# Block-recurrent cross attention and a token-mixing MLP in one kernel: a new operation order, a block diagonal written by small DMAs, and fewer dummy matmuls

## The chip, the cores and the metric

The kernel runs on one core of a Trainium2 chip. The metric is the device time of one execution in microseconds (us); a profile's span is 1.7 to 2.2 us shorter than the time of the same execution (88.75 and 87.0 us in the profiled run before). The kernel before takes 88.36 us (median of 3 runs, 88.14 to 88.51). Runs of one kernel scatter: an execution is called slow when it lies over 1.5% above the fastest of its kernel, and ratios use the others, the fast ones.

## The reference, cut to what matters

```python
# x: (8 batches, 8 heads, 512 tokens, 64), state: (8, 8, 32, 64), all float32
scores  = scale * x @ state^T ; a  = softmax(scores)  ; xread = a  @ state   # tokens read the state
scores2 = scale * state @ x^T ; a2 = softmax(scores2) ; sread = a2 @ x       # the state reads the tokens
y = heads side by side of concat([xread, sread], tokens)    # (8, 544, 512)
wq = y @ w_q ; wk = y @ w_k                                 # (8, 544, 64)
out = relu(scale2 * (wq @ wk^T) @ y) @ w_out                # (8, 544, 512)
```

The kernel never forms `y`. It uses `wq (wk^T y)`: a 64 x 512 matrix `V` per batch, whose block-diagonal factors `stbd` (the state) and `sbd` (the state's read) appear below.

## The kernel before

One long list, `ORDER`, fixes the order in which the operations are issued; each token is operation, batch, and engine or tile mode (`v` VectorE, `a` ACT, which is ScalarE, `p` GpSimd; `t`, `c`, `r`: one 128-column matmul, two of 64 columns, four of 32). The parts that the change and the argument touch:

```python
def load(n, b, e):                     # "ix3": batch 3's x, 512 KB as bf16, asked for by GpSimd
    if n == "iwo":
        nc.gpsimd.dma_start(out=w_o, in_=moe_w_out.rearrange("(k p) e -> p k e", p=128))
    # ... "is": the state of batches 3 to 7
    else:
        b = int(n[2:])
        nc.gpsimd.dma_start(out=x_bf[b], in_=xsrc(b, 0, H))

def fill(n, b, e):                     # b dummy matmuls that cover waits
    ps = psA.tile([128, 512], FP, name="fill_ps", tag="psA")
    for w in range(b):
        nc.tensor.matmul(out=ps, lhsT=zero[:, 0:128], rhs=zero, start=True, stop=True)

def stbd_blk(n, b, e):                 # block diagonal of one batch's state, on GpSimd
    for r in range(2):
        nc.gpsimd.tensor_tensor(out=stbd[:, b, r],
            in0=st_bf[:, b, r : r + 1, :].to_broadcast((128, NP, D)),
            in1=mask[:, :, None].to_broadcast((128, NP, D)), op=ALU.mult)

def sw_mm(n, p, e):                    # state times w_q and w_k, 64 rows contracted
    # ... for bb, q, r:
        nc.tensor.matmul(out=ps[NS * q : NS * q + NS, r, 2 * DH * bb : 2 * DH * bb + 2 * DH],
            lhsT=stT[64 * r : 64 * r + 64, 2 * p + bb, r, NP * r + q, :],
            rhs=w_qk[64 * r : 64 * r + 64, q, 0:2, :], start=True, stop=True)

def srd(n, b, e):                      # the state's read: 32 matmuls of 32 columns each
    for r in range(2):
        for c in range(NC):
            for q in range(NP):
                nc.tensor.matmul(out=L[b]["srd"][NS * q : NS * q + NS, r, 0:D],
                    lhsT=L[b]["E"][:, r, c, q, :],
                    rhs=x_bf[b][:, NP * r + q, D * c : D * c + D],
                    start=False, stop=(r == 1 and c == NC - 1), skip_group_check=True)
```

Other names used below: `xT` transposes x, `pt` are the scores, `at` transposes the normalised scores `A`, `mix` and `mixs` are the mixed tokens and state rows, `fin` and `fix` the output matmuls of the tokens, `fs` those of the state rows of four batches.

The softmax here doesn't subtract the row's maximum and nothing guards it: scores larger than these inputs give would overflow.

Of the kernel before, what the change touches and what calls it, by code (L numbers as in the profile page):

```python
# [8 lines left out]
FP = mybir.dt.float32  # L9
# [31 lines left out]
wke.6.a wqe.6.v mix1.5.r ve.4.a mixs.5.r mix0.5.r mxe1.5.v sums.3.t mxe0.5.a g.6.t srd.3.r mixs.4.r
# [6 lines left out]
mse.0.a wke.7.v fin0.6.c wqe.7.a mxe0.3.a g.7.c fin1.6.c ge.7.a fin0.3.c oe0.6.v fin1.3.c os0.6.s  # L48
v.7.c oe0.3.a fin2.3.c ve.7.a fin3.3.c os0.3.s mix0.7.r oe1.3.a mixs.7.r fs.3.t mxe0.7.v mse.7.a
os1.3.s mix1.7.r fse.3.v fs.7.t mxe1.7.a fse.7.v fix1.7.t fix2.7.t oc1.7.a fix0.7.t oc2.7.a fix3.7.t  # L50
oc0.7.a oc3.7.b
"""


@with_exitstack
def kernel(
# [9 lines left out]
    nc = tc.nc  # L66
# [601 lines left out]
```

## Time and profile before

| | before |
|---|---|
| time, median of 3 | 88.36 us |
| span of the profiled run | 87.0 us |
| TensorE busy | 93% of the span |
| TensorE's share of the chain that ended last | 90% |
| matmuls plus weight loads in the profile | 3151 |
| dummy matmuls in `ORDER` | 23 |

The chain is the work followed back from the last instruction, at each step to what released it. The prediction below shows the lines that carry this and says how to read them. One row also belongs here. It stands in the page's table of DMA queues (queue, kind: packets, megabytes, share of 16 engines' span):

```profile
q8 instruction: 12, 0.20, 0.9%
```

Instructions come by DMA too: 12 packets of 16,384 B in the whole run. With a share of 0.9% they look like nothing.

### The profile page before, as it was taken

The numbers are of one execution on the slowest core, as the hardware profiler recorded it, in microseconds if no ns is written. First come the engines' busy times: TensorE is split into PE (matmuls) and PEld (weight loads), VectorE is DVE, ScalarE is ACT, GpSimd is POOL, SyncE is SP. The second block draws the span as 40 slices with busy tenths as digits, with TensorE's granted clock in tenths as the row PEclk, the third lists the DMA queues.
The fourth block names the chain that finished last, engine by engine and source line by source line (L and its number), as shares of the span: only waits on it lengthen the run. The fifth ranks groups of instructions, "written<-read, shape, count | busy, mean of one in ns | idle before, by whom it ended". The sixth has DMA issues, their size and how long they took to land.

```text
span 87.0 us, 3553 instructions
## 1 busy us (share of the span) xinstructions
PE 80.8 (93%) x1572; PEld 53.4 (61%) x1579; DVE 52.4 (60%) x111; ACT 55.9 (64%) x83; POOL 45.1 (52%) x58
## 2 busy tenths in 40 slices
PE   4999999999999999999999999999999999999910
PEld 1326666878777778777689747866755565544400
DVE  2125793997956875897856957891688264056010
ACT  1541637999898858778797838967930592665530
POOL 7999948999999969408507735327150000000000
PEclk9999999999999999999999999999999999999996
DMA  0899999999609999995600464201461663566782
GB/s 12 292 312 187 202 191 198 195 165 147 96 0 121 143 128 277 322 169 72 241 8 4 171 281 175 115 8 53 188 243 45 275 281 136 213 269 277 294 314 80
DMA packets 15119, 15.00 MB, mean 172 GB/s; under 512 B 3712, under 2 KB 12672, under 8 KB 15104
## 3 DMA queue, kind: packets, MB, share of 16 engines
q0 software_dynamic: 9104, 4.36, 39.7%
q1 hardware_dynamic: 4880, 8.98, 28.0%
q10 hardware_dynamic: 1120, 1.44, 4.6%
q8 instruction: 12, 0.20, 0.9%
q14 instruction: 3, 0.02, 0.1%
HBM read 10.22 MB, written 8.91 MB: 220 GB/s over the span
## 4 chain that ended last, share of the span: by engine, by line
PE 90%; ACT 4%; issue 1%; DVE 1%
PE fin_ps L161 20%; PE fin_ps L163 12%; PE fill_ps L155 6%; PE xT_ps L174 5%; PE mix_ps L541 5%; PE warm_ps L132 4%; PE srd_ps L369 3%; PE xT_ps L170 3%; PE at_ps L174 3%; PE v_ps L505 3%; PE pt_ps L163 2%; PE g_ps L163 2%; PE fins_ps L163 2%; PE wq_ps L433 2%; PE v_ps L514 2%; PE wk_ps L163 2%
## 5 line engine op out<-in xcount | busy, mean ns | idle before, releaser
L346 POOL TENSOR_TENSOR A<-E,rinv 128x1024 bf16<-128x1024 bf16 (+1 forms) x9 | 15.4, 1717 | 12.8 <-DVE rinv L340 12.5
L161 PE MATMUL fin_ps<-w_o,rmix 128*64 128x512 bf16 x160 | 19.4, 380 | 0.0
L142 ACT COPY ost<-fin_ps 128x1024 f32<-128x1024 f32 (+2 forms) x13 | 11.2, 864 | 11.6 <-PE fin_ps L161 5.9
L148 ACT ACTIVATE rmix<-mix_ps 128x1024 bf16<-128x1024 f32 x12 | 12.1, 1024 | 2.4 <-PE mix_ps L541 2.4
L407 POOL TENSOR_TENSOR sbd<-srn,mask 128x256 bf16<-128x256 bf16 x16 | 9.4, 614 | 6.0 <-DVE srn L397 5.9
L144 DVE COPY ost<-fin_ps 128x1024 f32<-128x1024 f32 (+1 forms) x6 | 6.5, 1091 | 9.9 <-PE fin_ps L163 5.4
L161 PEld LDWEIGHTS <-rmix 128*64 128x64 bf16 x160 | 8.4, 110 | 6.2 <-issue 0.6
L332 DVE TENSOR_REDUCE rsum<-E 128x16 f32<-128x512 bf16 x16 | 10.8, 676 | 0.9 <-ACT E L317 0.6
L163 PE MATMUL fin_ps<-w_o,rmix 128*128 128x512 bf16 x44 | 11.0, 379 | 0.2
L317 ACT ACTIVATE E<-pt_ps 128x512 bf16<-128x512 f32 x16 | 9.5, 601 | 2.5 <-PE pt_ps L161 1.3
L142 ACT COPY xT<-xT_ps 128x1024 bf16<-128x1024 bf16 x7 | 7.1, 1012 | 4.6 <-PE xT_ps L174 3.9
L234 POOL TENSOR_TENSOR stbd<-st_bf,mask 128x256 bf16<-128x256 bf16 x16 | 9.3, 610 | 0.4 <-DVE st_bf L144 0.2
L155 PE MATMUL fill_ps<-zero 128*128 128x512 bf16 x21 | 7.8, 432 | 0.1
L144 DVE COPY xT<-xT_ps 128x1024 bf16<-128x1024 bf16 x9 | 6.2, 690 | 2.7 <-PE xT_ps L174 2.5
L150 DVE TENSOR_SCALAR rmix<-mix_ps 128x1024 bf16<-128x1024 f32 x4 | 4.9, 1222 | 3.4 <-PE mix_ps L541 3.4
L163 PEld LDWEIGHTS <-rmix 128*128 128x128 bf16 x48 | 4.3, 98 | 4.0 <-ACT rmix L148 0.2
L183 POOL DMA_DIRECT2D x_bf<-in_x_dram x7 | 6.6, 949 | 0.0
L174 PE MATMUL xT_ps<-ident,x_bf 128*128 128x128 bf16 x80 | 6.0, 219 | 0.2 <-ACT E L317 0.2
L174 PEld LDWEIGHTS <-x_bf 128*128 128x128 bf16 x80 | 5.1, 98 | 1.3 <-issue 0.5
L541 PE MATMUL mix_ps<-wq,V 64*128 64x256 bf16 x64 | 5.8, 272 | 0.0
L132 PE MATMUL warm_ps<-zero 128*128 128x512 bf16 x8 | 3.6, 631 | 1.2 <-DVE mask L133 1.2
L163 PE MATMUL pt_ps<-stT,xT 128*128 128x64 bf16 x88 | 4.4, 193 | 0.0
(90 smaller groups left out, 139.7 us busy)
## 6 DMA issues: line engine op xcount, KB each, us to landing
out_dram<-ost SPq DMA_DIRECT2D x14, 512.0 KB, 2.8
x_bf<-in_x_dram POOLq DMA_DIRECT2D x7, 512.0 KB, 7.8
out_dram<-ost ACTq DMA_DIRECT2D x3, 256.0 KB, 2.1
x_f<-in_x_dram ACTq DMA_DIRECT2D x2, 256.0 KB, 4.0
x_f<-in_x_dram SPq DMA_DIRECT2D x2, 256.0 KB, 4.4
w_o<-in_moe_w_out_dram POOLq DMA_DIRECT2D x1, 512.0 KB, 8.4
out_dram<-ost SPq DMA_DIRECT2D x2, 256.0 KB, 2.4
st_bf<-in_state_dram POOLq DMA_DIRECT2D x1, 160.0 KB, 7.8
```

The source lines that it names most:

```text
L142: nc.scalar.copy(out=out, in_=in_)
L144: nc.vector.tensor_copy(out=out, in_=in_)
L148: nc.scalar.activation(out=out, in_=in_, func=AF.Relu)
L155: nc.tensor.matmul(out=ps, lhsT=zero[:, 0:128], rhs=zero, start=True, stop=True)
L161: nc.tensor.matmul(out=out[64 * h : 64 * h + 64], lhsT=lh, rhs=rhs, **kw)
L163: nc.tensor.matmul(out=out, lhsT=lhsT, rhs=rhs, **kw)
L174: nc.tensor.transpose(out=out, in_=in_, identity=ident)
L317: nc.scalar.activation(out=L[b]["E"][:, r].rearrange("p c q n -> p c (q n)"), in_=L[b][f"pt{r}"], func=AF.Exp, scale=float(scale),)
L332: nc.vector.reduce_sum(out=L[b]["rsum"][:, w], in_=L[b]["E"].rearrange("p r c q n -> p (r c q) n")[:, w], axis=AX.X,)
L346: eng.tensor_tensor(out=L[b]["A"].rearrange("p r c q n -> p (r c q) n")[:, w], in0=L[b]["E"].rearrange("p r c q n -> p (r c q) n")[:, w], ...
L407: nc.gpsimd.tensor_tensor(out=L[b]["sbd"][:, r], in0=L[b]["srn"][:, r : r + 1, :].to_broadcast((128, NP, D)), in1=mask[:, :, None].to_broa ...
L541: nc.tensor.matmul(out=ps[:, h, kk, :], lhsT=L[b]["V"][rows, 128 * k : 128 * k + 128], rhs=L[b]["wq"][rows, 0:SH], start=True, stop=True,)
```

## The change

The intent is to take work off TensorE (fewer dummy matmuls, fewer changes of tile shape) and off GpSimd (the block diagonal of batches 1 to 7), in an order searched anew. The diff, with the order cut to its first lines:

```diff
 ORDER = """
-fill.7.t xT0.0.t xc2.0.v xTe0.0.a fill.1.t xT1.0.t is.0.p stc.1.v fill.1.t stt.1.c xTe1.0.v stbd.2.p
-fill.1.t pt0.0.t stf.1.v fill.1.t pt1.0.t exp0.0.a ste.1.v iwo.0.p exp1.0.a rs0.0.v fill.4.t
-sums.0.t ix3.0.p rinv0.0.v wc.0.a ...            # ix4 stands after stbd.1 and stbd.6
+fill.5.t xT0.0.t xc2.0.v fill.1.t xT1.0.t xTe0.0.v is.0.p xTe1.0.v fill.1.t pt0.0.t iwo.0.p exp0.0.a
+stc.1.v fill.1.t pt1.0.t ix3.0.p sbs.0.s fill.1.t stt.1.c exp1.0.a rs0.0.v stf.1.a rinv0.0.v
+fill.2.t sums.0.t rs1.0.v A0.0.p ...             # ix4 stands right after sbd.0
 ... (all further lines of the order differ)
+    nc.vector.memset(stT.bitcast(FP), 0.0)
     def zeros(n, b, e):
-        nc.gpsimd.memset(stT.bitcast(FP), 0.0)
+        nc.gpsimd.memset(stbd[:, 1:B].bitcast(FP), 0.0)
+
+    def stbd_put(n, g, e):                        # "sbs": the block diagonal by DMA
+        b0, b1 = ((1, 3), (3, B))[g]
+        for q in range(NP):
+            rows = slice(NS * q, NS * q + NS)
+            nc.sync.dma_start(out=stbd[rows, b0:b1, :, q, :], in_=st_bf[rows, b0:b1])
 ...
-                        lhsT=stT[64 * r : 64 * r + 64, 2 * p + bb, r, NP * r + q, :],
-                        rhs=w_qk[64 * r : 64 * r + 64, q, 0:2, :],
+                        lhsT=stT[:, 2 * p + bb, r, NP * r + q, :],
+                        rhs=w_qk[:, q, 0:2, :],
```

More of the change, by code (lines that the diff above doesn't have):

```diff
@@ L16 @@
 ORDER = """
-zst.0.p ix1.0.p stc.0.v xc1.0.a fill.1.t stt.0.c ste.0.v stbd.0.p stf.0.a xc0.0.p xc3.0.v ix2.0.p
-fill.7.t xT0.0.t xc2.0.v xTe0.0.a fill.1.t xT1.0.t is.0.p stc.1.v fill.1.t stt.1.c xTe1.0.v stbd.2.p
-fill.1.t pt0.0.t stf.1.v fill.1.t pt1.0.t exp0.0.a ste.1.v iwo.0.p exp1.0.a rs0.0.v fill.4.t
-sums.0.t ix3.0.p rinv0.0.v wc.0.a fill.1.t xT0.1.t rs1.0.v fill.1.t srd.0.r xTe0.1.v A0.0.p fill.1.t
-xT1.1.t fill.1.t sw.0.r xTe1.1.a rinv1.0.v fill.1.t pt0.1.t srn.0.v A1.0.p at0.0.t srT.0.t exp0.1.a
@@ L22 @@
-pt1.1.t srTe.0.v sbd.0.p swe.0.a xT0.2.t rs0.1.v at1.0.t exp1.1.a xT1.2.t xTe0.2.v stbd.1.p ate.0.a
-xTe1.2.v fill.1.t stt.2.c stt.3.c rs1.1.v ste.2.a pt0.2.t stbd.6.p stf.3.v exp0.2.a fill.1.t wq.0.c
-ste.3.v wks.0.c ix4.0.p stf.2.a wk.0.t rs0.2.v sw.3.r pt1.2.t wke.0.v swe.3.a stbd.3.p sw.1.r
-rinv.1.v exp1.2.a g.0.t sw.2.r ge.0.v stbd.5.p swe.1.a rs1.2.v sums.2.t v.0.c wqe.0.a rinv.2.v
-xT1.3.c swe.2.a A.1.p ve.0.v xT0.3.c xTe1.3.a srd.2.r xTe0.3.v mix0.0.r mix1.0.r mxe0.0.v sums.1.t
-mxe1.0.a A.2.p srd.1.r at.1.t pt1.3.t srn.1.v ate.1.a fin0.0.t srn.2.v ix5.0.p xT1.4.t exp1.3.a
@@ L28 @@
-srT.1.t xT0.4.t xTe1.4.v srTe.1.a fin1.0.t sbd.1.p xTe0.4.a rs1.3.v pt1.4.t wq.1.c sbd.2.p exp1.4.a
-wks.1.c wqe.1.v pt0.4.t oe0.0.a srT.2.t wk.1.t rs1.4.v at.2.t ix6.0.p fin2.0.t ate.2.v wke.1.a
-os0.0.s exp0.4.a stbd.7.p g.1.t srTe.2.v fin3.0.t ge.1.v rs0.4.v sums.4.t stbd.4.p oe1.0.a srd.4.r
-rinv.4.v v.1.c srn.4.v wq.2.c A.4.p ve.1.a os1.0.s srT.4.c wks.2.c wk.2.t srTe.4.a mixs.1.r wke.2.v
-mix1.1.r wqe.2.a mix0.1.r mse.1.v xT1.5.t mxe0.1.a ix7.0.p at.4.t xTe1.5.v g.2.t xT0.5.t mxe1.1.a
-ge.2.v sbd.4.p pt1.5.t xTe0.5.v v.2.c exp1.5.a fin2.1.c ve.2.v pt0.5.c rs1.5.v mixs.2.r mix1.2.r
@@ L34 @@
-exp0.5.a ate.4.v xT1.6.c mse.2.a sums.5.c fin3.1.c xTe1.6.a rs0.5.v rinv.5.v xT0.6.c mxe1.2.a
-oe1.1.v A.5.p pt1.6.c wq.4.c srd.5.r exp1.6.a mix0.2.r srn.5.v os1.1.s fin0.1.c mxe0.2.a rs1.6.v
-sbd.5.p xT0.7.c xTe0.6.v fin0.2.c xTe0.7.a wqe.4.v pt0.6.c srT.5.c at.5.c exp0.6.a xT1.7.c ate.5.v
-srTe.5.a fin1.2.c xTe1.7.a rs0.6.v wq.5.c rinv.6.v wks.5.c wk.5.c wqe.5.a pt1.7.c A.6.p wke.5.v
-wks.4.c sums.6.c exp1.7.a srd.6.r g.5.t oe0.2.a rs1.7.v wk.4.t pt0.3.t fin1.1.t srn.6.v exp0.3.a
-os0.2.s wke.4.v sbd.6.p at.6.t oe0.1.a rs0.3.v srT.6.t g.4.t fin2.2.t ate.6.v os0.1.s fin3.2.t
@@ L40 @@
-ge.5.v ge.4.v srTe.6.v v.5.c oe1.2.a rinv.3.v wq.6.c ve.5.v A.3.p wks.6.c wk.6.c v.4.c os1.2.s
-wke.6.a wqe.6.v mix1.5.r ve.4.a mixs.5.r mix0.5.r mxe1.5.v sums.3.t mxe0.5.a g.6.t srd.3.r mixs.4.r
-ge.6.v mix0.4.r mse.5.a mix1.4.r srn.3.v mxe0.4.a v.6.c mse.4.v sbd.3.p srT.3.c pt0.7.c srTe.3.v
-at.3.c mxe1.4.a ve.6.v fin2.5.c ate.3.v exp0.7.a fin3.5.c rs0.7.v wq.3.c oe1.5.a wks.3.c fin0.4.c
-rinv.7.v A.7.p wqe.3.a os1.5.s mix0.6.r mixs.6.r wk.3.t mse.6.a fin1.4.t wke.3.a mxe0.6.a g.3.t
-oe0.4.v at.7.t sums.7.t ate.7.a srd.7.r mix1.6.r srn.7.v os0.4.s fin2.4.c mxe1.6.v sbd.7.p srT.7.c
@@ L46 @@
-fin3.4.c srTe.7.a ge.3.v fin2.6.c oe1.4.v v.3.c fin3.6.c ve.3.v os1.4.s fin0.5.c oe1.6.a fin1.5.c
-os1.6.s mix1.3.r oe0.5.v mixs.3.r wq.7.c mxe1.3.a wks.7.c wk.7.c mixs.0.r mse.3.v mix0.3.r os0.5.s
-mse.0.a wke.7.v fin0.6.c wqe.7.a mxe0.3.a g.7.c fin1.6.c ge.7.a fin0.3.c oe0.6.v fin1.3.c os0.6.s
-v.7.c oe0.3.a fin2.3.c ve.7.a fin3.3.c os0.3.s mix0.7.r oe1.3.a mixs.7.r fs.3.t mxe0.7.v mse.7.a
-os1.3.s mix1.7.r fse.3.v fs.7.t mxe1.7.a fse.7.v fix1.7.t fix2.7.t oc1.7.a fix0.7.t oc2.7.a fix3.7.t
-oc0.7.a oc3.7.b
+zst.0.p ix1.0.p stc.0.v fill.1.t stt.0.c stbd.0.p xc1.0.a ste.0.v stf.0.v xc0.0.p xc3.0.v ix2.0.p
@@ new lines @@
+fill.5.t xT0.0.t xc2.0.v fill.1.t xT1.0.t xTe0.0.v is.0.p xTe1.0.v fill.1.t pt0.0.t iwo.0.p exp0.0.a
+stc.1.v fill.1.t pt1.0.t ix3.0.p sbs.0.s fill.1.t stt.1.c exp1.0.a rs0.0.v stf.1.a rinv0.0.v
+fill.2.t sums.0.t rs1.0.v A0.0.p fill.1.t srd.0.r fill.1.t xT0.1.t wc.0.a ste.1.v fill.1.t xT1.1.t
+rinv1.0.v fill.1.t at0.0.t xTe0.1.v A1.0.p xTe1.1.a fill.1.t sw.0.r srn.0.v fill.1.t pt0.1.t swe.0.v
+srT.0.t sbd.0.p at1.0.t exp0.1.a xT1.2.t ate.0.v srTe.0.a pt1.1.t xT0.2.t exp1.1.a xTe1.2.v wq.0.c
+sbs.1.s xTe0.2.a rs1.1.v stt.2.c stt.3.c ste.2.v wqe.0.a wks.0.c wk.0.t stf.3.a stf.2.v sums.1.t
@@ new lines @@
+srd.1.r ste.3.v ix4.0.p wke.0.a pt0.2.t pt1.2.t rs0.1.v exp0.2.a g.0.t sw.2.r ge.0.v exp1.2.a sw.3.r
+rinv.1.v v.0.c srn.1.v swe.2.a A.1.p sums.2.t rs1.2.v ve.0.a srd.2.r srT.1.t xT0.3.t srn.2.v
+srTe.1.a sw.1.r swe.3.a xTe0.3.v srT.2.t sbd.1.p at.1.t swe.1.a srTe.2.v pt0.3.t ate.1.v mixs.0.r
+mix1.0.r exp0.3.a ix5.0.p mix0.0.r mxe1.0.v xT1.3.c mxe0.0.a wq.1.c sbd.2.p wks.1.c wk.1.t mse.0.a
+xTe1.3.v fin0.0.t wke.1.a rs0.2.v pt1.3.t g.1.t wqe.1.v exp1.3.a xT0.4.t fin2.0.t rinv.2.v xTe0.4.a
+rs.3.v A.2.p fin1.0.t ge.1.a rinv.3.v pt0.4.t oe0.0.a fin3.0.t A.3.p at.2.t oe1.0.a os0.0.s sums.3.t
@@ new lines @@
+ate.2.v srd.3.r xT1.4.c exp0.4.a srn.3.v os1.0.s xT0.5.c ix6.0.p xTe1.4.v xT1.5.c xTe0.5.a wq.2.c
+sbd.3.p xTe1.5.v v.1.c wqe.2.a wks.2.c ve.1.v wk.2.t srT.3.t at.3.t wke.2.a srTe.3.v pt0.5.t g.2.t
+ate.3.v exp0.5.a mix0.1.r mixs.1.r mix1.1.r ge.2.v mxe0.1.a ix7.0.p wq.3.c mse.1.v mxe1.1.v wks.3.c
+v.2.c wqe.3.a pt1.5.c wk.3.t exp1.5.a pt1.4.t ve.2.v fin2.1.t exp1.4.a wke.3.v fin3.1.t rs.4.v
+sums.4.t g.3.t oe1.1.a sums.5.t xT1.6.t ge.3.v rinv.4.v mix1.2.r xTe1.6.v os1.1.s mix0.2.r A.4.p
+mxe1.2.a srd.5.r srd.4.r srn.5.v pt1.6.c xT0.6.c srn.4.v exp1.6.a srT.5.c fin0.1.c srTe.5.v sbd.5.p
@@ new lines @@
+mxe0.2.a xTe0.6.v xT0.7.c rs.5.v fin1.1.c xTe0.7.a sbd.4.p pt0.6.c srT.4.c xT1.7.c rinv.5.v oe0.1.a
+pt0.7.c A.5.p xTe1.7.v fin0.2.c exp0.6.a os0.1.s fin1.2.c srTe.4.a rs.6.v exp0.7.a sums.6.c fin2.2.c
+oe0.2.a rinv.6.v pt1.7.c A.6.p v.3.c exp1.7.a os0.2.s fin3.2.c ve.3.a rs.7.v sums.7.c oe1.2.a
+srd.7.r srd.6.r rinv.7.v mixs.3.r mixs.2.r mix1.3.r mse.3.a srn.6.v os1.2.s A.7.p mix0.3.r mse.2.a
+at.6.c mxe0.3.v mxe1.3.a fs.3.c ate.6.a at.5.c srn.7.v sbd.6.p fin2.3.c ate.5.v at.7.c fse.3.v
+sbd.7.p srT.7.c at.4.c ate.7.a srTe.7.v wq.5.c wks.5.c fin3.3.c wqe.5.v ate.4.a wq.7.c wks.7.c
@@ new lines @@
+oe1.3.a wk.7.c srT.6.c fin0.3.c wke.7.v srTe.6.a os1.3.s g.7.c fin1.3.c wqe.7.a ge.7.v wq.6.c
+oe0.3.a wks.6.c wk.6.c wqe.6.v v.7.c wke.6.v wk.5.c os0.3.s wq.4.c ve.7.v wke.5.a wks.4.c wk.4.t
+wqe.4.a g.5.t wke.4.v mix0.7.r ge.5.a mix1.7.r mxe0.7.a mixs.7.r g.4.t mse.7.v g.6.t ge.4.v v.5.c
+mxe1.7.v ge.6.a v.4.c ve.5.a v.6.c ve.4.v mix0.5.r ve.6.a mix1.5.r fix0.7.t mxe0.5.v mxe1.5.a
+fix1.7.t oc0.7.a mix0.4.r oc1.7.a mix1.4.r mixs.4.r fix2.7.t mxe1.4.v mxe0.4.a fix3.7.t oc2.7.a
+mse.4.a mix1.6.r oc3.7.v mix0.6.r fix2.4.t mxe0.6.a mxe1.6.v fix3.4.t oc2.4.v fin0.4.t oc3.4.b
@@ L52 @@
+fin1.4.t fin0.5.t oe0.4.a fin1.5.t os0.4.s fin0.6.t oe0.5.a fin1.6.t os0.5.s fin2.5.t oe0.6.a
+fin3.5.t os0.6.s fin2.6.t oe1.5.a fin3.6.t os1.5.s mixs.6.r mixs.5.r oe1.6.a mse.6.v mse.5.v fs.7.t
+os1.6.s fse.7.a
 """
@@ L625 @@
         "zst": zeros, "stt": st_tr, "ste": st_ev, "stf": st_ev,
-        "stbd": stbd_blk, "fill": fill, "fix": fin_mm, "os": fin_st,
+        "stbd": stbd_blk, "sbs": stbd_put, "fill": fill, "fix": fin_mm, "os": fin_st,
         "sw": sw_mm, "swe": sw_ev, "xT": xT_mm, "xTe": xT_ev, "xs": x_dT, "as": a_dT, "pt": pt_mm, "exp": pt_exp,
```

## The prediction

The stream is -1.08 (fills) - 1.28 (tile shapes) + 0.44 (state weights) = -1.9 us, the last group starts at 80.3 us instead of 81.86 with its wait of 0.75 counted in, thus -1.6, and 0.3 put down for the loads makes it -1.3, 87.1 us. The "release" is the start of the full clock: fills stand 0.43 us apart before it and 0.216 after. The 0.1 us of fixed cost of a reduction was an estimate; the trace after gives 0.12 (two of 512 elements 2 x 0.670 us, one of 1,024 1.217).

> **What bounds the kernel now.** I read four views in this order. First the busy times and the chain that ended last, at the head of the page:
>
> ```profile
> PE 80.8 (93%) x1572; PEld 53.4 (61%) x1579; DVE 52.4 (60%) x111; ACT 55.9 (64%) x83; POOL 45.1 (52%) x58
> ...
> PE 90%; ACT 4%; issue 1%; DVE 1%
> ```
>
> TensorE is busy 93% of the span and makes 90% of the chain, so a change counts only if TensorE has less to stream, waits less, or the tail after it shrinks. DVE, ACT and POOL (60, 64, 52%) are not the bound. Second, the TensorE timeline: the start of a group to the start of the next is its true cost, for the durations overlap.
>
> ```profile
> 42.59 1.03 PE L161 MATMUL fin_ps<-w_o,rmix 128*64 128x512 bf16 x8
> 43.45 0.42 PE L161 MATMUL pt_ps<-stT,xT 128*64 128x64 bf16 x16
> ...
> 59.02 1.03 PE L161 MATMUL fin_ps<-w_o,rmix 128*64 128x512 bf16 x8
> 59.98 0.39 PE L541 MATMUL mix_ps<-wq,V 64*128 64x256 bf16 x4
> ```
>
> The same eight output matmuls cost 0.86 us (43.45 - 42.59) where the next group has the same tile shape (128*64) and 0.96 us (59.98 - 59.02) where it changes to 64*128. I did this for all groups: a change of tile shape costs 0.09 to 0.11 us almost everywhere; I take 0.107.
>
> Third, the start, where dummy matmuls fill waits, and the end:
>
> ```profile
> 5.50 2.36 PE L155 MATMUL fill_ps<-zero 128*128 128x512 bf16 x7
> 7.70 0.61 PE L174 MATMUL xT_ps<-ident,x_bf 128*128 128x128 bf16 x8
> ...
> 79.26 3.62 PE L163 MATMUL fin_ps<-w_o,rmix 128*128 128x512 bf16 x16
> ```
>
> Seven fills take 2.20 us: the first cost about 0.43 each (cold clock), the last two 0.216. From 24.6 us on, TensorE loses about 0.3 us in all; the cold clock and the other waits lie before. The last of the four final groups starts 3 x 0.864 after 79.26, at 81.86 us; the span ends 5.1 us later (0.65 to its last matmul, 0.38 latency, copy, DMA, end).
>
> Fourth, GpSimd's timeline and the landings of the x loads:
>
> ```profile
> 15.44 2.33 POOL L234 TENSOR_TENSOR stbd<-st_bf,mask 128x256 bf16<-128x256 bf16 x4
> 17.71 0.94 POOL L183 DMA_DIRECT2D x_bf<-in_x_dram  x1
> ...
> DMA to landing us min/median/max: 5.7/7.8/10.0
> ```
>
> The block-diagonal multiplies stand before x loads in GpSimd's order, so they delay loads; they are not on the chain.
>
> [...] the fill at 5.90 us is followed by one 0.43 us later, that at 7.05 by one after 0.216; the release fell near 6.8 us here, 5.6 us after the first matmul. [...] five fills end where the sixth began, at 7.27 us. [...] 512 B packets of the x loads take a median of 60 ns, 4096 B output packets 159 ns, 256 B ones of the SyncE queue 18 ns.
>
> **The change part by part.** Counted in the two orders, with costs from the timeline (start to next start):
> - **Fills**: 23 to 18 dummy matmuls in the program, 5 x 0.216 = -1.08 us of TensorE stream. They are there to cover waits, so this is gain only where the data are in time.
> - **New order, tile shapes**: counting neighbours of different shape gives 58 changes before and 46 after: 12 x 0.107 = -1.28 us.
> - **Column-tiled state weights**: the 16 matmuls of a step contract 128 rows, half zero, in 128*32 tiles instead of 64*32. Before, a step costs 0.237 with the change that follows (19.20 to 19.44), so 0.13 without. The `srd` group streams the same number of columns (32 x 64 = 16 x 128) in the new shape, in 0.353 with a change, so 0.246. Estimate: 4 x 0.11 = +0.44 us; two of the four steps now stand together, which the count of 46 holds already.
> - **Block diagonal by DMA**: 14 multiplies x 0.61 = 8.5 us leave GpSimd; a memset of 1792 words stays there (2048 words took 1.80, so about 1.57). The one of 2048 words goes to VectorE: 256 words took 0.27 there, so about 2.1 us. It runs from 1.6 to 3.7 us, where VectorE waited for the state until 3.67: no cost. Added: 8 DMAs of 1792 packets of 128 B; at the 18 ns of a 256 B packet, 1792 x 18 / 16 = 2.0 us of the engines, in a time when x2, x3 and w_out move too.
> - **Merged row sums**: 5 fewer reductions on VectorE, each about 0.1 us of fixed cost: off the path.
> - **Evacuation** is about equal: ACT gets 4 output copies more and 3 relus and 2 transposes fewer; added up along the new order, neither ACT nor VectorE comes above three quarters of TensorE's work after 24 us.
>
> Sum of TensorE's stream, all groups and changes: 76.6 us before, 74.7 after, -1.9.
>
> **Where the waits are.** I walked the start by hand with the durations of the trace. New: transposes of x0 at 7.27 (cold clock, above), both their copies on VectorE, so the scores at 8.6 and 9.3, exp done at 10.3 instead of 11.2; x1 (landed 10.8) is waited for by nothing; the block with four copies and sums around 16 to 20 us keeps up. Output matmuls of batch 0 start at about 24.5 us, as before (24.58), but with 55.9 us of stream left instead of 57.8. So the start brings all of the 1.9 us: some of the removed fills did not cover waits but filled time in which other work can now run.
>
> New losses: at the very end the last group (state rows of batches 4 to 7) needs the `mixs` of batches 6 and 5 just before it: matmul to VectorE 0.29, two relus 0.68, back 0.05: it starts about 1.02 us after, instead of 0.27: +0.75 us. Then one copy and one 256 KB DMA; I get the same 5.1 us from the start of the last group to the end. Starting it at 24.5 + 55.0 + 0.75 = 80.3 against 81.86 gives -1.6 us. In the middle, x6 and x7 are now asked for at about 30.0 and 32.2 us (27.9 and 33.7 before), after the two normalisations. x5 took 7.3 us from an idle queue, and x7 landed 4.8 us after x6: they land at about 37.3 to 38.6 and 42.1 to 43.4; TensorE wants them at 38.7 and 42.0. I put down 0.3 us for that as the mean, since the loads may also be quicker. Net: -1.3 us, 88.36 to 87.1. The unit of the metric runs 1.4 us above the profile's span, in both.
>
> **Rivals.**
> - **All of it is gain** (-1.9 us or more, 86.4): the last group's wait is hidden and loads are early. For: GpSimd is 7 us freer, x4 is issued near 14.8 instead of 17.7, and the old trace shows a stream almost without waits after 24.6. Against: nothing stands between `mixs` and the last group.
> - **DMA becomes a wait** (87.8 to 88.5): the 128 B packets and the two outputs of batch 0 (issued near 29 and 30 us) hold up x3 (wanted at 20.8, landed 19.95 before), x5, x6 and x7. For: they were 7.3 to 8.9 us under way before. Against: small packets measured 18 ns, and the queue idles between loads.
> - **The fills covered waits** (88.4): the start is bound by x0's and x1's landing and TensorE stands still instead. Against: the walk above; x1 landed 0.9 us before it was used.
> - **An evacuation engine becomes the bound**: late chains of four batches run between 53 and 63 us with slacks of 0.1 to 0.5 us by my walk; a miss costs tenths.
>
> **Range and chances.** The stream is sure to about 0.3 us, the last wait to 0.2, the walk to 0.4, the loads to 0.5. Together some 0.8 us each way: 86.2 to 88.0. Faster by over 2% needs 86.59 or less, thus almost the first rival whole: 0.27. Slower by over 2% needs 90.1, over 3 us of new waits: 0.02.
>
> **What would show it.** In the new trace: TensorE's busy time down by about 2 us; a gap of 0.6 to 0.8 us ahead of the last `fins` group, ended by VectorE's relu of `mixs`; the first output group at about 24.5 us; `sw` groups at 0.35 us with a change; x6 and x7 landing at 37 to 43 us and TensorE's gaps ahead of their transposes. Wrong would be: idle TensorE before 20 us (the fills did cover waits), gaps ahead of x3 or x5, or a tail of more than 5.3 us after the start of the last group.

## The result and the profile after

The changed kernel takes 92.8 us (median of 4 runs, 91.95 to 93.76) against 88.25 us (4 runs, 87.77 to 88.51) for the kernel before. The ratio is 1.049, with a 95% interval of 1.040 to 1.058: slower by 5%. Here and below a ratio is the mean time of one kernel's fast runs over that of the other's fast runs of the same rounds, so it is not quite the ratio of the medians. The profiled run is a fast one (91.95 us, span 90.2).

The head of the page of the changed kernel, in the rows that answer to those shown of before, and the granted TensorE clock in 40 slices of the span, in tenths of full speed:

```profile
PE 80.8 (90%) x1557; PEld 54.2 (60%) x1562; DVE 53.0 (59%) x107; ACT 55.2 (61%) x84; POOL 36.9 (41%) x44
...
PEclk9999999999579999999999999999999999999995
...
q8 instruction: 12, 0.20, 0.9%
...
PE 58%; DMA 20%; POOL 6%; DVE 5%; issue 4%; ACT 2%; DVEq 0%; POOLq 0%
```

TensorE has fallen from 90 to 58% of the chain, and "issue" is 4%: time in which the engine at the end of the chain waited for nothing that the profile shows. The 20% of DMA are x loads, 9.00 us of them that of x6, through which the chain happens to run; TensorE's own wait for a load is 0.2 us, so the share is not a loss of that size. The clock row has a notch in slices 11 and 12 (22.5 to 27 us), which the kernel before has not. TensorE's own waits (what it waited for, us in total, times, longest):

```profile
PE srd_ps L375 <- issue: 2.4, 1, 2.4
PE warm_ps L131 <- DVE mask L132: 1.2, 1, 1.2
PE fins_ps L163 <- DVE rmix_s L150: 0.7, 1, 0.7
PE xT_ps L174 <- DMA x_bf<-in_x_dram: 0.2, 1, 0.2
```

The longest wait of the run is one that nothing released. TensorE's timeline shows where it stands (start, duration, line, operation, tile, shape, count, and in brackets the idle time before it):

```profile
20.07 0.35 PE L163 MATMUL srd_ps<-ones,E 128*128 128x1 bf16 x8
20.36 0.26 PE L375 MATMUL srd_ps<-x_bf,E 128*32 128x64 bf16 x10
23.00 0.51 PE L375 MATMUL srd_ps<-x_bf,E 128*32 128x64 bf16 x22 [2.38 <-issue]
23.44 0.29 PE L174 MATMUL srT_ps<-ident,srn 128*128 128x128 bf16 x1
23.52 1.06 PE L174 MATMUL xT_ps<-ident,x_bf 128*128 128x128 bf16 x8
...
28.31 0.38 PE L163 MATMUL fin_ps<-w_o,rmix 128*128 128x512 bf16 x1
...
84.74 1.04 PE L163 MATMUL fins_ps<-w_o,rmix_s 128*128 128x512 bf16 x4 [0.72 <-DVE rmix_s L150]
```

TensorE stops after the 10th of 32 like matmuls of one group, whose operands are all there, for 2.4 us, and goes on with the 11th. Then eight transposes take 0.99 us (23.52 to 24.51) instead of 0.55: half clock. Stages of the changed kernel give the granted clock (from:to, length, each engine's busy time, granted clock, DMA share, GB/s):

```profile
4.60:22.70 18.10, 15.74 (x343) 10.75 (x342) 12.54 (x28) 9.48 (x17) 11.89 (x15) 1.00 1.48 206
22.70:26.10 3.40, 3.10 (x58) 2.62 (x59) 1.45 (x4) 1.45 (x3) 2.18 (x4) 0.50 0.59 67
26.10:85.40 59.30, 58.14 (x1153) 39.59 (x1154) 36.59 (x65) 41.85 (x61) 18.99 (x18) 1.00 0.56 163
```

For 3.4 us the clock was halved; every run of the changed kernel has a mean clock of 0.963 to 0.967. The half clock of the tail takes 0.02 off that mean at most in these traces, and the notch another 0.019, so each run has such a notch. The first output group starts at 28.31 us, where it was predicted at 24.5.

### What the stop is

The stop falls at a round place. I counted TensorE's matmuls and weight loads in order of time: the stop stands after the 701st record, and after the 702nd in the traces that lack no record (e6, e9). Below it is called number 704, the round number next to it (3 x 256 - 64), and the other places are rounded in the same way. A packet of the instruction queue is 16,384 B, and 12 of them for some 3,120 recorded instructions make about 260 instructions each; as the stops below stand 255 or 256 records apart, I take 256. The second of the 12 was moved at 20.62 to 21.50 us, in the middle of the stop, and TensorE went on 1.5 us after it ended. (The texts call it the third fetch: they count the instructions that TensorE ran before the first of the 12 packets, which was moved at 14.57 us.) In the kernel before the same packet was moved at 18.72 to 19.61, and TensorE reached number 704 only at 22.15 us. The other packets of these two traces read alike: packet k starts between about 0.95 us before and 3.71 us after TensorE passes instruction 256k - 64 (the last one of the changed kernel 1.56 us before), and TensorE passes 256(k + 1) - 64 at the earliest 1.29 us after the packet has ended. So I count a packet as asked for at the first point, and take it that TensorE cannot pass the second without it; no packet was moved more than about one ahead of the block that TensorE was in. (The 64 is read off the traces, what it stands for is not shown, and a few records are missing.)

The trace's DMA packets, taken one by one, give this table for k = 2. "Asked" is when instruction 448 (record 446) ran, "lag" is from there to the start of the packet; all times in us. Here and below a stop runs from the start of the last instruction before it to the start of the next.

```
              asked   packet moved   lag    TensorE stops after 704   x3 landed   x4 asked for
before        18.22   18.72-19.61   0.50   no (704 reached 22.15)     19.95       17.71
after         17.27   20.62-21.50   3.35   20.43 to 23.00             20.91       14.48
```

Three things have moved. TensorE reaches 704 at 20.43 us instead of 22.15, so the packet is wanted earlier. The loads of x3 and x4 stand closer together: before, x4 was asked for only at 17.71, and two thirds of x3's 1,024 packets had begun when the instruction packet was asked for (under a quarter after); after, GpSimd is free of its multiplies and asks for x4 at 14.48. In both kernels x4's packets begin right behind x3's, at 19.4 us, but by 20.6 us 427 of them had begun instead of 213. And the small DMAs of the block diagonal (1,792 packets of 128 B) run in the same stretch, 13.37 to 23.54 us, x3 landing 1 us later. My first theory: **load traffic keeps the instruction fetch back, and the new order has no slack for it**. The rivals: the new order itself stalls there; or the stop has to do with the group of matmuls and not with the count.

### The profile page after: what moved, and what is told of

It reads as the page before. It is cut to its first block, busy times and chain, and to the rows that moved or that the text cites. A ratio compares the mean times of both kernels' runs of the same rounds, so it can differ in the third digit from the quotient of the medians.

```text
span 90.2 us, 3509 instructions
## 1 busy us (share of the span) xinstructions
PE 80.8 (90%) x1557; PEld 54.2 (60%) x1562; DVE 53.0 (59%) x107; ACT 55.2 (61%) x84; POOL 36.9 (41%) x44
## 4 chain that ended last, share of the span: by engine, by line
PE 58%; DMA 20%; POOL 6%; DVE 5%; issue 4%; ACT 2%; DVEq 0%; POOLq 0%
DMA x_bf<-in_x_dram 20%; PE fin_ps L163 16%; PE fin_ps L161 10%; POOL A L352 4%; PE mix_ps L547 4%; PE xT_ps L174 3%; PE srd_ps L375 3%; PE at_ps L170 2%; PE v_ps L511 2%; PE sw_ps L252 2%; POOL stbd L201 2%; PE xT_ps L170 1%; PE pt_ps L161 1%; PE at_ps L174 1%; PE v_ps L520 1%
## 5 line engine op out<-in xcount | busy, mean ns | idle before, releaser
L142 ACT COPY ost<-fin_ps 128x1024 f32<-128x1024 f32 (+2 forms) x17 | 15.3, 899 | 9.0 <-PE fin_ps L163 5.0
L163 PE MATMUL fin_ps<-w_o,rmix 128*128 128x512 bf16 x84 | 19.8, 380 | 0.2
L163 PEld LDWEIGHTS <-rmix 128*128 128x128 bf16 x88 | 8.1, 98 | 9.2 <-issue 0.4
L338 DVE TENSOR_REDUCE rsum<-E 128x16 f32<-128x512 bf16 (+1 forms) x11 | 10.1, 919 | 2.5 <-ACT E L323 2.4
L161 PE MATMUL fin_ps<-w_o,rmix 128*64 128x512 bf16 x80 | 10.3, 380 | 0.0
L148 ACT ACTIVATE rmix<-mix_ps 128x1024 bf16<-128x1024 f32 x9 | 9.4, 1042 | 1.3 <-PE mix_ps L547 0.8
L150 DVE TENSOR_SCALAR rmix<-mix_ps 128x1024 bf16<-128x1024 f32 x7 | 8.6, 1225 | 1.6 <-PE mix_ps L547 1.6
L375 PE MATMUL srd_ps<-x_bf,E 128*32 128x64 bf16 x256 | 3.4, 200 | 2.4 <-issue 2.4
L161 PEld LDWEIGHTS <-rmix 128*64 128x64 bf16 x80 | 4.3, 111 | 2.0
L144 DVE COPY AT<-at_ps 128x1024 bf16<-128x1024 bf16 x5 | 3.5, 692 | 2.8 <-PE at_ps L174 2.4
```

Source lines behind the costliest of these rows:

```text
L142: nc.scalar.copy(out=out, in_=in_)
L144: nc.vector.tensor_copy(out=out, in_=in_)
L148: nc.scalar.activation(out=out, in_=in_, func=AF.Relu)
L150: nc.vector.tensor_scalar(out=out, in0=in_, scalar1=0.0, scalar2=None, op0=ALU.max)
L161: nc.tensor.matmul(out=out[64 * h : 64 * h + 64], lhsT=lh, rhs=rhs, **kw)
L163: nc.tensor.matmul(out=out, lhsT=lhsT, rhs=rhs, **kw)
```

## The experiments

Fetch times and stops come from the one profiled run of each kernel; where that run was a slow one, it is said. Within a call the kernels share the runs of the kernel before; two calls may be on other chips (medians of before from 88.16 to 88.91 us), so compare ratios, not times, across calls.

### First call: what keeps the fetch back

**e1_late_x4**: x4 asked for about as late as before, by two scratch memsets on GpSimd ahead of it.

```diff
-srd.1.r ste.3.v ix4.0.p wke.0.a ...
+srd.1.r ste.3.v dly.0.p dly.0.p ix4.0.p wke.0.a ...
+    def delay(n, b, e):
+        nc.gpsimd.memset(scr, 0.0)          # scr: a new tile of 128 x 1792 words
```

> The changed kernel with two scratch memsets on GpSimd (about 3.1 us) ahead of the load of x4, so that it is issued at about 17.7 us as before the change instead of 14.5; all else as changed. Theory A (TensorE's third instruction fetch, started at 20.62 us, came late because the x4 load follows x3 in the GpSimd queue without a gap, so the fetch is served only after the x3 packets): the gap of 2.4 us in the srd.2 group disappears (under 0.5 us), the third fetch starts before 19.5 us, the clock stays at full rate, and the time is 87.5 to 89. Theory B (the 128-byte packets of the block-diagonal DMAs hold up the fetch or the loads): the gap stays at 2 us or more, time 91.5 to 93.

Measured: 90.49 us, ratio 1.0235 (1.013 to 1.034). The packet started at 19.86 (lag 2.53), the stop shrank to 20.49 to 22.16 (profiled run slow). Neither expectation was met: the stop is neither gone nor still 2 us. A second stop, at instruction 1728 and 43.6 us, appeared.

**e2_late_stbd**: the second group of small DMAs held back behind a second zeroing, after x5.

```diff
-sbs.1.s xTe0.2.a ...
+xTe0.2.a ...
-mix1.0.r exp0.3.a ix5.0.p mix0.0.r ...
+mix1.0.r exp0.3.a ix5.0.p zs2.0.p sbs.1.s mix0.0.r ...   # zs2: memset of stbd[:, 3:B] on GpSimd
```

> The changed kernel with the second set of block-diagonal DMAs (batches 3 to 7, 1280 packets of 128 B) held back until GpSimd has zeroed their destination again, behind the load of x5 (about 24 to 25 us); x4 still issued at 14.5. Theory A: the gap in srd.2 stays at 2 us or more, time 91.5 to 93. Theory B: the gap goes (under 0.5 us), time 87.5 to 89.5.

Measured: 92.53 us, ratio 1.0341 (1.021 to 1.048). The packet started at 20.47 (lag 3.44) and the stop took 2.8 us, in a profiled run that was slow; the fast runs, with a mean clock of 0.982 to 0.986, left no trace. These four DMAs alone do not keep the fetch back.

**e3_late_both**: both edits together.

> Both delays together. Theory A or B alone, or both needed: the gap in srd.2 is gone, full clock from 7 us on, time 87.3 to 89. If the gap of 2 us stays, neither the x4 load nor the second set of block-diagonal DMAs causes it, and both theories fall.

Measured: 90.12 us, ratio 1.0192 (1.007 to 1.031). The packet started at 19.75, the stop ran from 20.75 to 22.15, where both theories had it gone, and the clock was not halved:

```profile
PEclk9999999999999999999999999999999999999965
```

**e4_split_fills**: each dummy matmul of 512 columns as two of 256. The work is the same; 18 matmuls and 18 weight loads are added ahead of the stop. If the stop belongs to a count of instructions, it moves 36 instructions back; if to an operation or a transfer, it stays.

```diff
-        for w in range(b):
-            nc.tensor.matmul(out=ps, lhsT=zero[:, 0:128], rhs=zero, start=True, stop=True)
+        for w in range(2 * b):
+            c = slice(256 * (w % 2), 256 * (w % 2) + 256)
+            nc.tensor.matmul(out=ps[:, c], lhsT=zero[:, 0:128], rhs=zero[:, c], start=True, stop=True)
```

> The changed kernel with each of the 18 dummy matmuls of 512 columns split in two of 256: the same stream time, but 18 more weight loads and 18 more matmuls ahead of the gap. If TensorE stands still because its instructions have run out (fetch theory), the gap starts 18 matmuls earlier in the program: not after the 10th matmul of the srd.2 group but at the start of the sums.2 group, 8 matmuls ahead of it, and about 0.4 us earlier than 20.43 us. If the srd.2 matmuls wait for something of their own (data, a PSUM buffer, a DMA), the gap stays at the 11th matmul of srd.2. Time 91.5 to 94 either way.

Measured (one run): 94.05 us. TensorE's timeline:

```profile
19.50 0.39 PE L521 MATMUL v_ps<-stbd,G 128*64 128x256 bf16 x4
22.23 0.38 PE L164 MATMUL srd_ps<-ones,E 128*128 128x1 bf16 x8 [2.34 <-issue]
22.54 0.63 PE L376 MATMUL srd_ps<-x_bf,E 128*32 128x64 bf16 x32
```

The stop stands now before the eight row sums, exactly 18 matmuls earlier (8 sums and 10 of the next group), again after instruction 704 (record 702). It belongs to the count of instructions, not to an operand: as I read it, TensorE ran out of instructions.

### Second call: which part of the traffic

**e5_undo_dma**: the new order, but the block diagonal multiplied on GpSimd again, and the x loads behind those multiplies as before.

```diff
-... ix3.0.p sbs.0.s ...            +... stbd.2.p ix3.0.p ...
-sbs.1.s xTe0.2.a ...               +xTe0.2.a ...
-... ix4.0.p ...                    +... stbd.1.p stbd.6.p ix4.0.p ...
-... sbd.2.p ...                    +... sbd.2.p stbd.3.p stbd.5.p ...
-... ix7.0.p ...                    +... ix7.0.p stbd.7.p stbd.4.p ...
```

> The changed kernel with its new order, but the block diagonals of batches 1 to 7 made by GpSimd multiplies again (placed so that x3 is issued near 10 and x4 near 17.5 us), no small DMAs. If the small DMAs pushed x3 and with it TensorE's third instruction fetch back, x3 lands at about 20 us instead of 20.9 to 21.3, the fetch (asked for near 17.3 us) starts by 18.9 instead of 20.6, instructions are there about 1.45 us after its end, near 21.2, and the gap in srd.2 shrinks from 2.4 to 0.4 to 0.9 us without half clock; time 87.0 to 88.8. If the order alone (fewer long dummies, so 256 instructions are used up in 3.2 instead of 3.9 us) makes the gap, it stays at 1.5 us or more and the time at 90 or above.

Measured: 89.35 us, ratio 1.0029 (0.995 to 1.011). The packet started at 19.51 (lag 2.29); stops at 704 (20.50 to 21.87) and at 1728 (about 1.1 us) remain. The stop and the time lie between the two expectations: the small DMAs are part of the delay, not all of it.

**e6_all_stbd_late**: all eight small DMAs after x5, x4 late as in e1 (`zs2` here zeroes `stbd[:, 1:B]`).

```diff
-... ix3.0.p sbs.0.s ...            +... ix3.0.p ...
-sbs.1.s xTe0.2.a ...               +xTe0.2.a ...
-... ix5.0.p ...                    +... ix5.0.p zs2.0.p sbs.0.s sbs.1.s ...
-... ix4.0.p ...                    +... dly.0.p dly.0.p ix4.0.p ...
```

> The changed kernel with all eight small DMAs held back until after the x5 load (about 24 us), and x4 issued near 17.6 us by two scratch memsets. Against the run with both delays, only the first four small DMAs are gone from 9 to 18 us. If those hold x3 and the fetch back: x3 lands at 20 or earlier, fetch starts by 18.9, gap 0.3 to 0.9 us, time 87.5 to 89.5. If not: x3 at 21, gap 1.4 us, time 89.5 to 90.5.

Measured: 89.98 us, ratio 1.0077 (0.998 to 1.018). Packet at 19.07 (lag 2.17), stop at 704 of 1.2 us, again between the expectations; TensorE also waited 0.6 us for x6. Taking both DMA effects out of the way brings the kernel back to the old time, but not below it.

**e7_split_loads**: x3 to x7 in four DMAs each, so that one DMA holds 256 packets of 512 B instead of 1,024. (The 64 and 16 packets per engine below are these divided by the page's 16 engines; the trace does not tell a packet's engine.)

```diff
-            nc.gpsimd.dma_start(out=x_bf[b], in_=xsrc(b, 0, H))
+            w = H if b < 3 else H // 4
+            for h in range(0, H, w):
+                nc.gpsimd.dma_start(out=x_bf[b][:, h : h + w], in_=xsrc(b, h, h + w))
```

> The changed kernel with the loads of x3 to x7 each issued as four DMAs of two heads (256 packets, 16 for each of the 16 engines) instead of one of 1024 (64 for each engine); small DMAs and x4 as changed. Theory C: an instruction fetch waits on its engine for the end of the load's 64 packets there (64 x 60 ns = 3.8 us at most, lags of 2.2 to 3.6 us seen); with 16 packets at a time the lag falls under 1.5 us, both gaps (TensorE instruction 704 and 1726) go or stay under 0.5 us, time 87.3 to 89. If the lag stays above 2.5 us, the size of a load's batch is not what the fetch waits for, and the gap stays over 2 us, time 91.5 to 93.5.

Measured: 91.47 us, ratio 1.012 (1.003 to 1.021). Two of its four runs were slow, so its ratio rests on two. In the profiled run (slow) the packet lagged 3.80 us and the stop was 2.9 us. The two fast ones, at a mean clock of 0.994 and 0.995, cannot have had the notch, and no trace shows their fetches: what the split did in them is open.

**e8_split_and_late**: e7 with all small DMAs late, x4 early.

> Split loads and all small DMAs after x5 (no scratch memsets, x4 as early as changed). If either remedy works and they add: no gap over 0.4 us, full clock, time 86.8 to 88.2, the value that the sum of the stream asked for. If x4's early start alone keeps the fetch back in spite of both, the gap stays over 1.5 us.

Measured: 92.92 us, ratio 1.0465 (1.037 to 1.056). In a fast profiled run the packet lagged 3.55 us, the stop ran from 20.43 to 22.97. In e8 split loads do not help, and with all small DMAs gone from this stretch the fetch is kept back all the same, with x4 early. That speaks against the idea that one DMA's 64 packets per engine hold up the fetch as a block; e7's fast runs keep it from being settled.

### Third call: make room for the fetch

**e9_queue_gap**: x3 before the output weights, and these only at 17.3 us, so that GpSimd's queue is empty when the third fetch is asked for; otherwise e6.

```diff
-... iwo.0.p exp0.0.a ...                +... exp0.0.a ...
-... dly.0.p dly.0.p ix4.0.p ...         +... dly.0.p dly.0.p iwo.0.p ix4.0.p ...
```

> All eight small DMAs late as in e6_all_stbd_late, and now GpSimd asks for x3 ahead of the output weights and for these only after its two scratch memsets, near 17.6 us, then for x4: so GpSimd's queue runs empty about 17.5 us and has nothing new in flight before about 19 us, which covers the moment at which TensorE's third instruction fetch is asked for (16.9 to 17.3 us). If loads in flight keep that fetch back: it starts at 18.4 us or before (19.07 in e6, 20.62 in the changed kernel), TensorE doesn't stop after instruction 704 or for less than 0.4 us (1.2 in e6, 2.6 in the changed kernel), the clock isn't halved after 20 us, and the time falls 1.0 to 1.8 us below e6, ratio to before 0.985 to 0.997. If the fetch has a fixed latency of some 3 to 4 us after its request (counted from instruction 448) or the order itself is what costs, it starts at 19 us or later, the gap stays at about 1.2 us and the ratio at 1.00 to 1.015. The second gap, near instruction 1728 at 42 us, stays at about 1 us in both.

Measured: 90.86 us, ratio 1.0254 (1.012 to 1.039); profiled run slow. The fetch did what the theory says: asked for at 16.77, it started at 17.84 (lag 1.07 instead of 2.17), and the stop at 704 was 0.47 us. But the next fetch now met the output weights and x4 (lag 4.18): 1.0 us of stop after instruction 960, and 2.4 us after 1728 (lag 4.62). The time that I expected was wrong, for the account had left out where the traffic goes.

**e10_gap_early_x67**: e9 with x6 and x7 asked for before the normalisations of batches 2 and 3 (and no longer at their later places).

```diff
-rs.3.v A.2.p ... fin3.0.t A.3.p ...     +rs.3.v ix6.0.p A.2.p ... fin3.0.t ix7.0.p A.3.p ...
```

> e9_queue_gap with x6 and x7 asked for before, not after, the normalisations of batches 2 and 3 (about 26.5 and 28.5 us instead of 31 and 33), so that both have landed by about 38 us. If loads in flight keep fetches back: the fetch that TensorE asks for at instruction 1472 (about 36.5 us) starts within 1.5 us instead of 3.7 (e6), no gap of over 0.3 us at instruction 1728, and the time is another 0.6 to 1.2 us below e9, ratio to before 0.973 to 0.988, so up to the forecast of the prediction. What could take it back: the fetches asked for at 26 and 32 us now meet x6 and x7; they have about 2.5 us of slack, and a gap at instruction 1216 or 1472 would show a miss. If the second gap isn't from loads in flight, the ratio equals that of e9.

Measured: 90.65 us, ratio 1.0308 (1.023 to 1.039); profiled run slow. The expected 0.973 to 0.988 was missed. No stop at 1728, but stops after 960 (1.8 us), 1216 (1.0) and 1472 (1.4), with lags of 4.7, 6.1 and 4.7 us. (A lag counted from an instruction at which TensorE itself stood still takes that stop in; from its restart these are 4.3, 4.3 and 3.8 us.)

**e11_mixs_early**: e10 with the `mixs` of batches 6 and 5 one output group earlier.

```diff
-... fin3.6.t os1.5.s mixs.6.r mixs.5.r oe1.6.a mse.6.v mse.5.v fs.7.t
+... mixs.6.r mixs.5.r mse.6.v mse.5.v fin3.6.t os1.5.s oe1.6.a fs.7.t
```

> e10_gap_early_x67 with the mixs groups and relus of batches 6 and 5 moved ahead of the output group fin3.6, so that the last group doesn't wait for them. If the wait of 0.77 us ahead of the last group is what the prediction took it for, it is down to about 0.25 us, and the time falls 0.4 to 0.55 us below e10; if the end is set by something else (the last copy, the queue of output DMAs), it equals e10 within 0.15 us.

Measured: 90.06 us, ratio 1.026 (1.020 to 1.032), all runs fast. The waits of TensorE in its profile:

```profile
PE pt_ps L166 <- issue: 1.3, 1, 1.3
PE warm_ps L134 <- DVE mask L135: 1.2, 1, 1.2
PE wk_ps L166 <- issue: 1.0, 1, 1.0
```

The last group's wait is gone; the ratio is 0.005 below e10's, as expected but within the scatter. The stop at 704 is gone as well (lag 0.83); those after 960 and 1472 are the two "issue" rows. In these three kernels every stop of 0.4 us or more that nothing released, after 12 us, stands after 704, 960, 1216, 1472 or 1728 (records 702, 957, 1213, 1468, 1724: 255 or 256 apart).

### Fourth and fifth call: is the predicted gain there without late fetches?

**e12_no_late_loads** and **e13_before_no_late_loads**: the changed kernel and the kernel before without the loads of x3 to x7. Batches 3 to 7 compute on batch 2's data, so the result is wrong (relative error 0.07 in both).

```diff
-    x_bf = [const.tile([128, H, NC * D], BF, name=f"x_bf{b}") for b in range(B)]
+    x_bf = [const.tile([128, H, NC * D], BF, name=f"x_bf{b}") for b in range(3)]
+    x_bf += [x_bf[2]] * (B - 3)
-            nc.gpsimd.dma_start(out=x_bf[b], in_=xsrc(b, 0, H))
+            if b < 3:
+                nc.gpsimd.dma_start(out=x_bf[b], in_=xsrc(b, 0, H))
```

> The changed kernel without the loads of x3 to x7: batches 3 to 7 compute on the data of batch 2, so the result is wrong on purpose; the instructions of TensorE, ACT and VectorE are the same. If TensorE's stops come from its instruction fetches waiting behind load traffic, every fetch from the third on starts within 1 us of its request, no stop over 0.3 us stands at instructions 704, 960, 1216, 1472 or 1728, the clock isn't halved before the tail, and the time is near the forecast of the prediction: ratio to before 0.975 to 0.990, and 0.980 to 0.990 of e13 (the kernel before without the same loads). If the new order itself makes TensorE slower (operand waits or fetches that are late without any load), the ratio stays above 1.00 and above e13's.

> The kernel before without the loads of x3 to x7 (wrong result on purpose in the same way). The trace of before shows no stop of TensorE for instructions with these loads in flight, so both theories expect it within 1% of the kernel before: ratio 0.990 to 1.003. It is there so that the change can be compared without load traffic: e12 over e13 is the worth of the order, the fills and the tile shapes alone, by the prediction about 87.1/88.36 = 0.986.

Measured: e12 87.97 us, ratio to before 0.9995 (0.992 to 1.007); e13 88.94 us by the median of all four runs, but two of them are slow; its fast ones are 87.58 and 88.27, and e12's mean is 1.001 of theirs. So taking the loads away takes the 5% away: from 1.049 to 1.00. It does not bring the forecast 0.986, nor the 0.975 to 0.990 expected here. The waits in e12's trace:

```profile
PE warm_ps L132 <- DVE mask L133: 1.2, 1, 1.2
PE fins_ps L164 <- DVE rmix_s L151: 0.7, 1, 0.7
PE srd_ps L377 <- issue: 0.4, 1, 0.4
```

There is still a stop of 0.6 us after 704: with the small DMAs in flight (the last landed at 20.55 us) the packet took 1.55 us (17.95 to 19.50) instead of about 0.9. In e13 no packet from the second on lags over 0.83 us, and TensorE never stops for instructions.

**e14_best_try**: a correct kernel with what helped: e5 (multiplies on GpSimd, x4 late), x6 at 26 us, `mixs` early.

```diff
 (from e5)
-... sbd.2.p stbd.3.p stbd.5.p ...       +... sbd.2.p stbd.3.p ix6.0.p ...
-... xT0.5.c ix6.0.p ...                 +... xT0.5.c ...
-... ix7.0.p stbd.7.p stbd.4.p ...       +... ix7.0.p stbd.5.p stbd.7.p stbd.4.p ...
 (and the edit of e11)
```

> e5_undo_dma (block diagonal multiplied on GpSimd again, x4 asked for late) with x6 asked for at about 26 us instead of 31, the multiplies of batch 5 moved after x7, and the mixs of batches 6 and 5 before the last group but one, as in e11. If the second stop (instruction 1728) comes from x6 and x7 in flight, it shrinks from about 1.1 to under 0.5 us and no other appears, and the last wait of 0.7 us goes: the ratio to before falls from 1.003 to 0.982 to 0.992. The first stop of about 1.3 us at instruction 704 stays. If the fetch of instruction 1216 or 1472 meets x6 instead, a stop of about 1 us stands there and the ratio is 0.993 to 1.003.

Measured: 87.70 us, ratio 0.9947 (0.986 to 1.003): the best correct version, not shown to beat the kernel before. The second stop and the last wait are gone (fetch at instruction 1472: lag 1.30); one row is left, and the expected 0.992 was just missed:

```profile
PE srd_ps L377 <- issue: 0.7, 1, 0.7
```

**e15_no_late_dma_mixs**: e12 (wrong) with the small DMAs late as in e6 and the `mixs` of e11.

> e12_no_late_loads (wrong on purpose) with all small DMAs after batch 5's place in GpSimd's order, as in e6, and the mixs of batches 6 and 5 moved up, as in e11. e12's trace has TensorE's stream end 2.3 us after an undisturbed start would let it: 0.6 of it is a last stop at instruction 704 behind the small DMAs, 0.77 the last group's wait, the rest the cold clock and short waits of the start. If these terms are the whole account, the stop is under 0.2 us, the wait about 0.25, the last group starts at 79.4 to 79.8 us instead of 80.67, the span is 84.4 to 84.9 us (85.7 in e12) and the ratio to before 0.980 to 0.992: the predicted gain is there when no fetch is late. If the ratio stays at 0.995 to 1.005, something else eats the gain.

Measured: 87.45 us, ratio 0.9922 (0.985 to 0.9997), all four runs fast. No stop over 0.2 us is left, and the end of TensorE's timeline is without the old wait:

```profile
78.44 0.36 PE L573 MATMUL mixs_ps<-wq,V 64*128 64x32 bf16 x8
78.73 1.04 PE L165 MATMUL fin_ps<-w_o,rmix 128*128 128x512 bf16 x4
79.61 1.03 PE L165 MATMUL fins_ps<-w_o,rmix_s 128*128 128x512 bf16 x4
```

The last group starts at 79.61 us, as expected (79.4 to 79.8). The span is 85.1, not 84.4 to 84.9, because the tail behind that group took 5.5 us here. So with its instructions in time and the last wait gone, the new order is ahead by just under 1%, with an interval that almost touches 1. That is less than half of the 1.9 us (2.2%) that the sum of the stream promised without that wait; where the rest went is said below.

### The steps together

| kernel | ratio to before | stop at 704, us | others |
|---|---|---|---|
| changed kernel | 1.049 | 2.6 | 0.2 at 1728 |
| x4 late (e1) | 1.024 | 1.7 | 1.5 at 1728 |
| x4 and four small DMAs late (e3) | 1.019 | 1.4 | 1.1 at 1728 |
| x4 and all small DMAs late (e6) | 1.008 | 1.2 | 1.0 at 1728 |
| block diagonal on GpSimd (e5) | 1.003 | 1.4 | 1.1 at 1728 |
| the same, x6 earlier, no last wait (e14) | 0.995 | 0.9 | none |
| no loads of x3 to x7 (e12) | 1.000 | 0.6 | none |
| no loads, small DMAs late, no last wait (e15) | 0.992 | 0.2 | none |

(Intervals are about 0.01 to either side, so neighbours need not differ.)

## Why the prediction was wrong

**What bounds the kernel: right, as far as it went.** TensorE was and is the engine that counts. But a TensorE that loses little was taken for one that nothing else could hold up. In the kernel before, the packet in question ended at 19.61 us and TensorE came to its end of supply at 22.15; since after the two stops of the changed kernel, at 704 and 1728, it went on only 1.50 and 1.35 us after the packet ended, some 1.1 us of that was to spare, by estimate. A faster TensorE uses up such slack by being faster.

**The sum of TensorE's stream: right.** I added up the predicted costs along both orders and laid them beside the traces. In e12, where little disturbs it, from the first `fin` to the last group the sum was 55.0 us and the trace 55.85, of which 0.77 is the last wait. An `sw` group took 0.35 us with its change of shape, as said. In the kernel before, that stretch, from its first `fin` to its last group, took 57.27 us, so the shorter stream is real. The sign named for it, "TensorE's busy time down by about 2 us", did not show: 80.8 us in both, some 1.1 us of it at half clock. Without late loads it is 80.3 in e13, 79.2 in e12 and 78.7 in e15.

**The last group's wait: right**, 0.77 us measured for 0.75. **x6: right in size, partly by luck.** TensorE lost 0.35 us to it, for 0.3; but it was 9.0 us under way (33.84 to 42.84), not 7.3 to 8.6, and TensorE came to it later than forecast because of the stop.

**The start: here it failed.** The step is "I walked the start by hand with the durations of the trace" and "Output matmuls of batch 0 start at about 24.5 us": they started at 28.31. Counted back from 24.5 by the sum of the stream, the walk agrees to about 0.1 us with the trace at 20.07 us, the start of the last group before the stop. That is partly luck: the transposes of x0 ran at 6.63 us, not 7.27, since the trace's record of full clock begins at 5.6 us here and at 6.9 before, the scores at 8.16 and 8.85, not 8.6 and 9.3; by 20 us waits had used up this lead. The walk asked of every operation whether its operands were there; it never asked whether the instructions were. The account of the 3.8 us, by the difference between the trace and the sum: 2.73 us at the stop, 1.1 us in the three groups after it that ran at half clock (0.44, 0.21 and 0.41). The half clock began inside the stop, at 22.70 us, and lasted 3.41 us. Not every stop was followed by it. By the clock rows of the traces the clock was halved after the stops of 2.6 us (changed kernel), 2.3 to 2.9 us (e2, e4, e7, e8; e2 and e7 in slow runs) and 1.7 us (e1, a slow run), and not after those of 1.2 to 1.4 us (e3, e5, e6), nor after those of 2.4 us (e9) and 1.8 us (e10, both slow runs). The changes of the clock lie 17.07, 3.41 and 61.44 us apart in the changed kernel and 78.51 us in the kernel before, each a whole multiple of 3.41. What tells the stops apart is not shown.

**The rest.** From the first `fin` to the last group the trace has 56.43 us for the predicted 55.75 (waits for PSUM tiles and for x6, 0.2 to 0.35 each), and the tail 5.42 for 5.1, which is over the 5.3 that the prediction named as a sign of being wrong. Predicted span 85.7, plus 3.8, 0.7 and 0.3, less the 0.3 that had been put down for the loads: 90.2, the measured span. The "1.4 us above the profile's span" was a slip: it set the median (88.36) against the span of a profiled run that itself took 88.75. It stood on both sides of the forecast difference.

**The rivals.** "DMA becomes a wait" named the right traffic (x3, the 128 B packets) and the wrong victim: x3 landed at 20.91 us, about when it would have been wanted, and cost next to nothing; the instruction fetch behind the same packets cost most of the 5%. "Small packets measured 18 ns, and the queue idles between loads" was the argument against it; the packets of 128 B took a median of 26 ns, and the queue that had to idle was the one in front of the fetch (with a gap in it, in e9, the lag was 1.07 us instead of 2.17). "All of it is gain" was off in a second way that e15 shows: with no stop and no last wait it is 0.8%, not 2.2%. By the same sum TensorE has lost 1.0 us in e15 by the first `fin`, the stop left out, and 0.4 us in e13: with fewer dummy matmuls, short waits of the start lie open (0.3 us twice for the casts of x0, in e15), so "the fills covered waits" holds in part. And the tail behind the sum's end took 4.6 us in e15 and 4.1 in e13; the prediction had it equal.

**What stays open.** That late fetches stop TensorE is shown by e4 and by the stops 255 or 256 recorded instructions apart. That traffic makes them late is shown by e9 and e11 (a gap in the queue: lag 2.2 in e6, 1.07 and 0.83 there) and by e12. How the DMA engines let a queue of loads go before an instruction packet is not shown: e8 speaks against the length of one DMA, and e7 leaves it open. The lags behind loads were 2 to 4.6 us, against 0.50 us for the packet in question in the kernel before and 0.83 us at most, from the second packet on, in e13.

## What to carry to other kernels

Before you speed up an engine with thousands of short instructions, count its instructions and look up in the trace when each packet of them came and when it was needed: here TensorE wanted 16 KB by DMA every 256 instructions, and they came late while loads were in flight (3.35 us after they were asked for in the changed kernel). The waits that the profile gave to "issue" in the midst of equal instructions, at the same count modulo 256 (after 704, 960, 1216, 1472 and 1728), were such late fetches. If you find one while loads are in flight, move the load and keep the small DMAs out of that stretch, which took the ratio from 1.049 to 1.008 in e6 (leaving the dummy work in may also do, but was not tried alone); and then see which fetch meets the load in its new place.
